# 126 tiny reads placed between the large loads of a memory-bound decode block

## The chip, the core and the metric

The kernel runs on one core of a Trainium2 chip. The metric is the device time of one execution in microseconds (us). Before the change it is 235.2 us, the median of two runs (235.15 and 235.26). Loads from the chip's memory (HBM) into the on-chip buffer are carried out by the core's 16 DMA engines; the engines that issue them here are SyncE (SP) and, for two small reads at the start, ScalarE (ACT). TensorE (PE) multiplies matrices, VectorE (DVE) transposes and does elementwise work, GpSimd (POOL) does a few copies.

## The reference

One decode step of a transformer block with modulation by a condition `c`, for a batch of 2, one new position each, model width 512, 32 query heads over 8 key/value heads of 128, the last W = 4096 positions of a cache of 32768, and a feed-forward width of 1792, all in float32:

```
mod = (silu(c) @ w_mod) in six parts sa, ca, ga, sb, cb, gb
h = layernorm(x) * (1 + ca) + sa
q = (h @ wq) as 32 heads;   k, v = k_cache, v_cache[:, :, 32768 - 4096 :, :]
p = softmax(q k^T / sqrt(128));   o = p v
x = x + ga * (o @ wo)
h = layernorm(x) * (1 + cb) + sb
x = x + gb * (silu(h @ w1) @ w2)
```

w_mod has 6 MB, wq 8 MB, the parts of the key and the value cache that are used 32 MB each, wo 8 MB, w1 and w2 3.5 MB each (MB here of 1024 KB). Every byte is used once.

## The kernel before

All operations are first recorded by `Flow.record`, which notes for each which earlier ones it depends on (by the regions of the on-chip tensors that it reads and writes); `Flow.emit` then issues them in the order in which they were written, each engine for itself, with a wait on a semaphore where a dependence needs one. Each DMA has its own semaphore, which is raised by 16 when it has landed. So the order of the loads is that of the code, on SP's queue, and a load whose buffer is still in use makes SP wait, and with it everything behind it on SP.

Nearly all loads go into one large tensor, `store`. Its first 32768 columns are four slots of 8192 (4 MB each). w_mod lies in slot 3 and the columns behind it, wq in slots 0 and 1. Keys and values come in eight steps t (four pairs of key/value heads by two batch rows, `seq`): the load k_t brings the keys of two heads, v_t the values, 4 MB each, with one packet of 32 KB to each of 128 partitions. The order of these sixteen loads is k0, k1, v0, k2, v1, k3, v2, ... k7, v6, v7 (`order`, line 470), and load i goes to slot (i + 2) mod 4 (`place`). `fetch(n)` issues the loads up to the n-th; the loop at line 487 calls it between the stages, so that a load is written behind the work that frees its slot:

```
for t in range(NP + 1):
    if t < NP:
        scores(t)          # DVE transposes k_t (4 x), PE multiplies, softmax
        fetch(max(5, 2 * t + 4))
    if t > 0:
        values(t - 1)      # PE multiplies the probabilities with v_(t-1)
        fetch(2 * t + 5)
    if t < NP:
        probabilities(t)
```

Behind the loop come wo in two parts (6 MB and 2 MB, called wo and wo2 below), w1 (3.5 MB) and w2 in four parts (2 MB, 1 MB and two of 256 KB). wo goes to slots 2 and 3, w1 to slot 0, w2 to slot 1. Their products (`product`, `narrow`) follow one another: o @ wo, the second layernorm, h @ w1, silu, the product with w2, and the store of the result.

At the end of `emit`, SP waits for all engines, clears the semaphores and waits for the last DMA.

Of the kernel before, what the change touches and what calls it, by code (L numbers as in the profile page):

```python
# [31 lines left out]
class Flow:  # L32
# [25 lines left out]
    def record(self, engine, method, args, kw):  # L58
        aps = [(k, v) for k, v in (*enumerate(args), *kw.items()) if isinstance(v, bass.AP)]
        outs = {0, "out", "accum_out"} if 0 in dict(aps) else {"out", "accum_out"}  # L60
        me = len(self.ops)
        needs = set()
        for writes in (False, True):
            for k, ap in aps:
                if (k in outs) != writes or "dram" in ap.tensor.name:
                    continue
                r = self.region(ap)
                held = self.seen.setdefault(ap.tensor.name, [])
                for other, w, o in held:
                    if (w or writes) and other != me and (  # L70
                        r[0] < o[1] and o[0] < r[1] and r[2] < o[3] and o[2] < r[3]
                    ):
                        needs.add((other, w))
                if writes:
                    held[:] = [
                        x for x in held
                        if not (r[0] <= x[2][0] and x[2][1] <= r[1] and r[2] <= x[2][2] and x[2][3] <= r[3])
                        or x[0] == me
                    ]
                held.append((me, writes, r))  # L80
        if engine == "pool":

            needs |= {(i, True) for i, o in enumerate(self.ops) if o[0] == "pool"}
        self.ops.append((engine, method, args, kw, needs))

    def emit(self):
        nc, ops = self.nc, self.ops
        proc = [("dma", i) if o[1] == "dma_start" else o[0] for i, o in enumerate(ops)]
        known = {e: {} for e in self.NAMES}
        after, waits, told = [], [], set()  # L90
        for i, (engine, method, _, _, needs) in enumerate(ops):
            mine, wait = known[engine], []
            for d, wrote in sorted(needs, reverse=True):
                p = proc[d]
                if p == engine and (engine == "pe" or not wrote):
                    continue
                if mine.get(p, -1) >= d:
                    continue
                wait.append(d)
                told.add(d)  # L100
                for q, n in after[d].items():
                    mine[q] = max(mine.get(q, -1), n)
                mine[p] = max(mine.get(p, -1), d)
            waits.append(wait)
            after.append(dict(mine))
        sems = {e: nc.alloc_semaphore(f"at_{e}") for e in self.NAMES}
        done = nc.alloc_semaphore("done")
        count = {e: 0 for e in self.NAMES}
        value, last = {}, None
        for i, (engine, method, args, kw, _) in enumerate(ops):  # L110
            eng = getattr(nc, self.NAMES[engine])
            for d in waits[i]:
                eng.wait_ge(*value[d])
            ins = getattr(eng, method)(*args, **kw)  # L114
            if method == "dma_start":
                last = nc.alloc_semaphore(f"dma{i}")
                ins.then_inc(last, 16)
                value[i] = (last, 16)
            elif i in told:
                count[engine] += 1  # L120
                ins.then_inc(sems[engine], 1)
                value[i] = (sems[engine], count[engine])

        for e in ("pe", "dve", "act", "pool"):
            getattr(nc, self.NAMES[e]).sem_inc(done, 1)
        nc.sync.wait_ge(done, 4)
        first = min(s.num for s in sems.values())
        nc.sync.sem_clear(range(first, last.num))
        nc.sync.wait_ge(last, 16)
        nc.sync.sem_clear(last)  # L130


def adaln_block(nc, x, k_cache, v_cache, wq, wo, w1, w2, c, w_mod, out):
# [7 lines left out]
    pe, dve, act, pool, sp = fl.pe, fl.dve, fl.act, fl.pool, fl.sp  # L141
# [6 lines left out]
    def buf(name, *shape):  # L148
        return nc.alloc_sbuf_tensor(name, list(shape), F32).ap()
# [36 lines left out]
    def load_cache(cache, t, where):  # L186
        hp, b = seq[t]
        sp.dma_start(
            where,
            cache[b, 2 * hp : 2 * hp + 2, SK - W :, :].rearrange(  # L190
                "u (i n) d -> i u (n d)", n=NK
            ),
        )
        return where
# [149 lines left out]
    for n in range(2):  # L344
# [4 lines left out]
        for g in range(G):  # L349
            r = slice(32 * g, 32 * g + 32)  # L350
            eng = pool if g % 2 else dve
# [7 lines left out]
        for i in range(4):  # L359
            r = slice(32 * i, 32 * i + 32)  # L360
# [115 lines left out]
    def fetch(n):  # L476
        for i in range(fetched[0], min(n, len(order))):
            what, t = order[i]
            if what == "k":
                kt[t] = load_cache(k_cache, t, place[i])  # L480
            else:
                vt[t] = load_cache(v_cache, t, place[i])
        fetched[0] = max(fetched[0], n)

    fetched = [0]
    fetch(4)
    for t in range(NP + 1):
        if t < NP:
            scores(t)
            fetch(max(5, 2 * t + 4))  # L490
        if t > 0:
            values(t - 1)
# [4 lines that stand above are left out]
    def load_rows(w, per, lo, hi, s, at):  # L497
        e = w.shape[1]
        n = (hi - lo) * e
        sp.dma_start(s[:, at : at + n], w.rearrange("(p q) e -> p (q e)", q=per)[:, lo * e : hi * e])  # L500
        v = s[:, at : at + n].rearrange("p (q e) -> p q e", e=e)
        return {q: v[:, q - lo, :] for q in range(lo, hi)}
# [2 lines left out]
    WIDE = 24  # L505
    for lo, hi in ((0, WIDE), (WIDE, 32)):
        wot |= load_rows(wo, 32, lo, hi, store[:, 2 * SLOT : 4 * SLOT], lo * D)
    w1t |= load_rows(w1, 4, 0, 4, slot[0], 0)
    for lo, hi in ((0, 8), (8, 12), (12, 13), (13, 14)):
        w2t |= load_rows(w2, T2, lo, hi, slot[1], lo * D)  # L510
# [143 lines left out]
```

## Time and profile before

| | |
|---|---|
| time, median of 2 runs | 235.2 us |
| profiled execution: whole time | 235.42 us |
| profiled execution: span from the first to the last instruction | 234.0 us |
| moved by DMA | 97.68 MB, 417 GB/s on the mean |
| busy share of the span: PE, DVE, ACT | 61%, 49%, 12% |
| chain of work that ended last: DMA, DVE, PE | 61%, 23%, 13% |

How to read it: the chain is followed back from the last instruction, at each step to what released it. A DMA's issue is an instruction of SP with a time of its own; its landing is seen when the semaphore is raised. "Packets" are the pieces that the DMA engines carried; the views on DMA count those under 512 bytes, under 2 KB and under 8 KB, and give the time that the packets of a queue took as a share of 16 engines' time in the window asked for. Queue q1 is SP's, q10 ACT's; q8 and q14 bring instructions. The packets carry no number of the engine that moved them.

### The profile page before, as it was taken

How to read it: one execution, taken by the hardware profiler on the slowest of the kernel's cores; microseconds unless marked ns; L12 is line 12 of the kernel's file. 1: busy time of each engine (PE TensorE's matmuls, PEld its weight loads, DVE VectorE, ACT ScalarE, POOL GpSimd, SP SyncE). 2: the span in 40 equal slices, each digit the busy share in tenths (PEclk: the TensorE clock that was granted, in tenths of full speed). 3: DMA queues.
4: the chain of work that ended last, by engine and by line, in shares of the span. 5: the costliest groups of instructions: out<-in, count | busy, mean ns of one | idle time of the engine just before them, and what ended most of it. 6: DMA issues, size and time to landing. Idle time of an engine off the chain costs nothing.

```text
span 234.0 us, 2450 instructions
## 1 busy us (share of the span) xinstructions
PE 143.0 (61%) x1070; PEld 41.8 (18%) x1070; DVE 113.9 (49%) x155; ACT 27.7 (12%) x62; POOL 8.1 (3%) x27
## 2 busy tenths in 40 slices
PE   0013905918458756995457755737664777859885
PEld 0001301211001200231100210200220022313425
DVE  4014100179497596794295477549429560200331
ACT  2003000010110120221200210120120030000500
POOL 4600000000000000000000000000000000000000
PEclk9999975895755997799955999797997697998999
DMA  7999998999999999999999999999999999989992
GB/s 269 438 516 392 403 493 358 445 431 420 426 433 437 437 434 420 431 423 437 448 420 420 434 431 437 437 416 431 428 448 431 426 442 437 437 384 447 407 412 79
DMA packets 3646, 97.68 MB, mean 417 GB/s; under 512 B 412, under 2 KB 436, under 8 KB 692
## 3 DMA queue, kind: packets, MB, share of 16 engines
q1 hardware_dynamic: 3612, 97.52, 97.3%
q8 instruction: 8, 0.13, 0.2%
q14 instruction: 2, 0.02, 0.0%
q10 hardware_dynamic: 24, 0.01, 0.0%
HBM read 97.53 MB, written 0.00 MB: 417 GB/s over the span
## 4 chain that ended last, share of the span: by engine, by line
DMA 61%; DVE 23%; PE 13%; issue 1%; ACT 1%; POOL 0%; SPq 0%; POOLq 0%
DMA store<-in_A_k_cache_dram 35%; DVE kT L114 19%; DMA store<-in_A_wq_dram 15%; DMA store<-in_A_wo_dram 11%; PE bankD L114 8%; PE bankA L114 3%; PE bankC L114 1%; DVE store L114 1%; PE bankB L114 1%; DVE qbd L114 0%; ACT store L114 0%; DVE wide L114 0%; DVE sgh L114 0%; DVE mx L114 0%; DVE hidT L114 0%
## 5 line engine op out<-in xcount | busy, mean ns | idle before, releaser
L114 DVE STREAM_TRANSPOSE kT<-store 128x2048 f32<-128x2048 f32 x32 | 71.1, 2279 | 15.6 <-DMA store<-in_A_k_cache_dram 15.5
L114 PE MATMUL bankA<-kT,qbd 128*32 128x512 f32 x256 | 49.6, 854 | 32.4 <-DVE kT L114 32.3
L114 PE MATMUL bankD<-store 128*32 128x512 f32 x256 | 33.7, 673 | 2.6 <-DMA store<-in_A_v_cache_dram 2.6
L114 PEld LDWEIGHTS bankA<-kT,qbd 128*32 128x32 f32 x256 | 6.2, 124 | 69.6 <-DVE kT L114 68.8
L114 PE MATMUL bankD<-store,hq_T 128*32 128x512 f32 x64 | 9.4, 752 | 8.6 <-DMA store<-in_A_wq_dram 8.6
L114 PEld LDWEIGHTS bankD<-store 128*32 128x32 f32 x256 | 8.6, 122 | 20.7 <-issue 20.6
L114 ACT COPY bias<-bankB 128x1 f32<-128x1 f32 x8 | 1.3, 159 | 91.4 <-PE bankB L114 91.4
L114 DVE STREAM_TRANSPOSE store<-store 128x512 f32<-128x512 f32 x8 | 5.7, 712 | 12.2 <-ACT store L114 12.2
L114 DVE TENSOR_REDUCE mx<-bankA 128x1 f32<-128x512 f32 x8 | 5.5, 692 | 12.2 <-PE bankA L114 12.2
L114 PE MATMUL bankB<-mv_a,avg 128*128 128x1 f32 x2 | 0.6, 363 | 16.7 <-DVE mv_a L114 16.7
L114 DVE TENSOR_TENSOR store<-store,half 128x512 f32<-128x512 f32 x16 | 10.3, 689 | 0.3
L114 DVE STREAM_TRANSPOSE wide<-bankD 128x512 f32<-128x512 f32 x2 | 1.4, 718 | 16.9 <-PE bankD L114 16.9
L114 PE MATMUL bankO<-store,pick 128*32 128x256 f32 x32 | 7.7, 382 | 2.9 <-ACT store L114 2.9
L114 PE MATMUL bankC<-store,sel 128*32 128x256 f32 x64 | 7.5, 414 | 3.1 <-DVE store L114 3.1
L114 ACT ACTIVATE store<-bankC,par 128x256 f32<-128x256 f32 x16 | 7.6, 475 | 10.9 <-PE bankC L114 10.7
L114 PE MATMUL bankD<-store,oTn 128*32 128x512 f32 x48 | 7.1, 750 | 2.9 <-DMA store<-in_A_wo_dram 2.9
L114 PE MATMUL bankC<-qbd,mean 128*128 128x512 f32 (+1 forms) x18 | 8.3, 591 | 0.0
L114 ACT COPY store<-bankD 128x512 f32<-128x512 f32 x8 | 4.7, 585 | 28.2 <-PE bankD L114 28.2
L114 DVE STREAM_TRANSPOSE aoT<-bankA 128x128 f32<-128x128 f32 x1 | 0.3, 316 | 14.0 <-PE bankA L114 14.0
L114 PE MATMUL bankB<-ident,mx 128*1 128x128 f32 x16 | 3.0, 271 | 6.5 <-DVE mx L114 6.5
L114 DVE BATCH_NORM_STATS2 st_a<-x_sp 128x6 f32<-128x128 f32 x1 | 0.3, 294 | 12.4 <-DMA x_sp<-in_A_x_dram 12.4
L114 PE MATMUL bankB<-negscale,mrow 1*128 1x1 f32 x16 | 3.4, 279 | 4.7 <-DVE mrow L114 4.7
(115 smaller groups left out, 91.0 us busy)
## 6 DMA issues: line engine op xcount, KB each, us to landing
store<-in_A_k_cache_dram SPq DMA_DIRECT2D x8, 4096.0 KB, 29.9
store<-in_A_v_cache_dram SPq DMA_DIRECT2D x8, 4096.0 KB, 29.0
store<-in_w_mod_dram SPq DMA_DIRECT2D x1, 6144.0 KB, 17.4
store<-in_A_wo_dram SPq DMA_DIRECT2D x1, 6144.0 KB, 25.0
store<-in_B_w_dram SPq DMA_DIRECT2D x1, 3584.0 KB, 30.8
store<-in_A_wo_dram SPq DMA_DIRECT2D x1, 2048.0 KB, 29.5
store<-in_B_w_dram SPq DMA_DIRECT2D x1, 2048.0 KB, 30.3
store<-in_B_w_dram SPq DMA_DIRECT2D x1, 1024.0 KB, 31.0
```

The costliest lines, as they stand in the source:

```text
L114: ins = getattr(eng, method)(*args, **kw)
```

## The change

A small tensor `small` of 16 partitions is added, and a function `read_small` that issues fourteen reads of the first words of `c` into it: the read with r rows (r = 2 to 15) brings r rows of r + 1 float32 words, so 12 to 64 bytes a row. Nothing reads `small`. The function is called nine times: in `fetch` after every second one of the sixteen loads of keys and values (after k1, k2, k3, ..., k7 and v7), and once between wo2 and w1. That makes 126 reads with 9 x 119 = 1071 rows, all on SP's queue.

The reads are kept out of the tracking of dependences (`record`) and share one semaphore, `tiny`. In `emit`, the first read of each group of fourteen, but for the first group, waits until all earlier tiny reads have landed; and at the end SP waits for all 126.

```diff
@@ record
-                if (k in outs) != writes or "dram" in ap.tensor.name:
+                if (k in outs) != writes or "dram" in ap.tensor.name or ap.tensor.name == "small":
@@ emit
+        tiny, tinies = nc.alloc_semaphore("tiny"), 0
...
             for d in waits[i]:
                 eng.wait_ge(*value[d])
+            if method == "dma_start" and args[0].tensor.name == "small" and tinies and tinies % 14 == 0:
+
+                eng.wait_ge(tiny, 16 * tinies)
             ins = getattr(eng, method)(*args, **kw)
-            if method == "dma_start":
+            if method == "dma_start" and args[0].tensor.name == "small":
+                ins.then_inc(tiny, 16)
+                tinies += 1
+            elif method == "dma_start":
...
         nc.sync.wait_ge(done, 4)
+        nc.sync.wait_ge(tiny, 16 * tinies)
@@ fetch
                 vt[t] = load_cache(v_cache, t, place[i])
+            if i % 2 == 1:
+                read_small(i // 2)
...
+    small = buf("small", 16, 14, 16)
+    cf = c.rearrange("b d -> (b d)")
+
+    def read_small(t):
+        for rows in range(2, 16):
+            n = 1 + rows
+            sp.dma_start(
+                small[:rows, rows - 2, :n],
+                cf[: rows * n].rearrange("(r n) -> r n", n=n),
+            )
@@ before w1
+    read_small(8)
     w1t |= load_rows(w1, 4, 0, 4, slot[0], 0)
```

On SP's queue, before, the part from k2 to k4 reads as follows (`store<-in_A_k_cache_dram` is a load of keys, `in_A_v_cache_dram` one of values; the shape is that of the target; a wait stands in brackets, `at_pe` and `at_dve` being the waits for PE and DVE to free the slot):

```order
5 L114 DMA store<-in_A_k_cache_dram 128x1x8192 [waits at_pe]
6 L114 DMA store<-in_A_v_cache_dram 128x1x8192 [waits at_dve]
7 L114 DMA store<-in_A_k_cache_dram 128x1x8192 [waits at_dve]
8 L114 DMA store<-in_A_v_cache_dram 128x1x8192 [waits at_pe]
9 L114 DMA store<-in_A_k_cache_dram 128x1x8192 [waits at_dve]
```

and now the part from the end of the group behind k2 to the first three reads of the group behind k3 (eleven more follow before v2):

```order
32 L118 DMA small<-in_c_dram 14x15
33 L118 DMA small<-in_c_dram 15x16
34 L118 DMA store<-in_A_v_cache_dram 128x1x8192 [waits at_dve]
35 L118 DMA store<-in_A_k_cache_dram 128x1x8192 [waits at_dve]
36 L118 DMA small<-in_c_dram 2x3 [waits tiny]
37 L118 DMA small<-in_c_dram 3x4
38 L118 DMA small<-in_c_dram 4x5
```

Between k3 and v2 (rows 7 and 8 before) there are now fourteen issues, and the first of them holds SP until the group behind k2 has landed; v2 and all later loads stand behind that wait. At the end of the loads SP had this before (`in_B_w_dram` is w1 in the first such row, then w2):

```order
18 L114 DMA store<-in_A_wo_dram 128x12288 [waits at_dve]
19 L114 DMA store<-in_A_wo_dram 128x4096
20 L114 DMA store<-in_B_w_dram 128x7168 [waits at_pe]
21 L114 DMA store<-in_B_w_dram 128x4096 [waits at_pe]
22 L114 DMA store<-in_B_w_dram 128x2048 [waits at_pe]
```

and has this now, up to the second read of the last group (twelve more follow, then w1):

```order
129 L118 DMA small<-in_c_dram 15x16
130 L118 DMA store<-in_A_wo_dram 128x12288 [waits at_dve]
131 L118 DMA store<-in_A_wo_dram 128x4096
132 L118 DMA small<-in_c_dram 2x3 [waits tiny]
133 L118 DMA small<-in_c_dram 3x4
```

w1 and w2 have moved behind the last group, whose first read waits for the group issued behind v7. On PE, DVE, ACT and POOL the instructions and their order are the same as before.

## The prediction

> **What bounds the kernel now.** I read the page's DMA part first, then the chain of waits, the windows around single loads, and SP's timeline. The page's part on DMA, with packets and megabytes by queue:
>
> ```profile
> DMA packets 3646, 97.68 MB, mean 417 GB/s; under 512 B 412, under 2 KB 436, under 8 KB 692
> q1 hardware_dynamic: 3612, 97.52, 97.3%
> q8 instruction: 8, 0.13, 0.2%
> q10 hardware_dynamic: 24, 0.01, 0.0%
> ```
>
> SP's queue keeps the 16 DMA engines busy for 97.3% of the span; there is almost nothing to win between loads. The chain (start, length, what):
>
> ```profile
> 74.64 22.65 DMA store<-in_A_k_cache_dram
> 106.22 29.93 DMA store<-in_A_k_cache_dram
> 183.95 25.01 DMA store<-in_A_wo_dram
> ```
>
> These give landings: k3 at 97.29, k5 at 136.15, wo at 208.96. From k3 to k5 four loads landed in 38.86 us, 9.72 us each, and 4.19 MB in 9.72 us is 432 GB/s. k5 was issued 29.93 us before its landing, three load times, so about two whole loads stood ahead of it: the ring never ran dry. At that pace wo's 6.29 MB took 14.6 us, so v7 landed at about 194.4; wo2 (2.10 MB, 4.9 us) at 213.8.
>
> The last wait for a load, from the timeline:
>
> ```profile
> 222.42 0.16 PEld L114 LDWEIGHTS bankA<-store,hT_b 128*32 128x32 f32 x8 [0.77 <-DMA store<-in_B_w_dram]
> ```
>
> PE waits for w1 at 222.42; from there to the end of the span are 11.6 us of dependent work. What delays w1's landing comes out at the end in full.
>
> A load lands when its latest engine has finished. Two windows of the DMA view, 16.85 to 17.76 us (the end of w_mod) and 191.5 to 194 us (the end of v7), show the completions, one small packet for each engine:
>
> ```profile
> DMA packets 32, 1.05 MB, mean 1152 GB/s; under 512 B 16, under 2 KB 16, under 8 KB 16
> ...
> DMA packets 46, 1.33 MB, mean 531 GB/s; under 512 B 16, under 2 KB 16, under 8 KB 16
> ```
>
> and the part of the second from 193 to 194 us holds five of them:
>
> ```profile
> DMA packets 16, 0.54 MB, mean 541 GB/s; under 512 B 5, under 2 KB 5, under 8 KB 5
> ```
>
> So all 16 finish w_mod within 0.91 us, but v7 only within 2.5 us, the last five in the last 1.0. The engines drift apart. The 8 instruction packets on q8 fit as one cause (0.2% of 16 x 234 us over 8 is 0.9 us each, on one engine at a time). Most engines are thus one to two microseconds early, and delay on those costs nothing.
>
> **The change part by part.** *Packets added.* A large load makes 128 + 16 packets: 25 x 144 = 3600 of q1's 3612; the remaining 12 are the result's store, eight rows with four completions, and q10's 24 are the reads of c and x, twice the same. A small DMA's rows thus come with fewer than 16 completions. I take a read of r rows as spread over r engines, with one data packet and one completion on each, a "pair". A group of fourteen then gives 14 pairs to an engine that every read touches, down to none for one that no read touches, 7.4 on the mean (119/16); nine groups give at most 126 and on the mean 67.
>
> *Price of a pair.* The trace has two nearby packets: a 4-byte completion (window 10.05 to 10.07 us) and a 512-byte row of c or x (window 6.38 to 6.40 us):
>
> ```profile
> q10 hardware_dynamic: 1, 0.00, 2.8%
> ...
> q10 hardware_dynamic: 1, 0.00, 8.4%
> ```
>
> 2.8% of 16 x 20 ns is 9 ns; 8.4% is 27 ns. The added rows have 12 to 64 bytes, nearer to 4 than to 512, so I take 9 ns, and 18 ns a pair; the ends are 0 (completions between large loads leave the pace at 432 GB/s) and 9 + 27 = 36 ns. On an engine with 126 pairs that is 2.3 us (0 to 4.5), with 67 pairs 1.2 us. Behind eight of the nine groups wo still waits; all nine precede w1.
>
> *What reaches the end.* If the latest engine carries none, the 2.3 us on the busiest one fit within the 2.5 us of spread: nothing. If the latest carries all 126, 2.3 us. The trace does not name engines. With 67 pairs on the latest it is 1.2 us, and as the second latest may carry more, I take 1.5 us. Below nothing: at best a delay of the early engines lets the late ones catch up, which is worth no more than the spread, 2.5 us.
>
> The Trainium skill (DMA: Bandwidth & Descriptors, "Anatomy of one DMA") speaks against the change: it gives every DMA a fixed cost of about 2.0 us. If that were paid in turn, 126 x 2.0 = 252 us would come on top, an estimate of 487 us by that page; the same section says that most of it is the wait for the write's receipt. The trace does not bear out a cost in turn: 25 large loads end in such a completion at an unbroken 432 GB/s.
>
> *SP's time.* Issues, from SP's timeline:
>
> ```profile
> 0.74 0.39 SPq L114 DMA_DIRECT2D store<-in_w_mod_dram  x1
> 74.64 0.54 SPq L114 DMA_DIRECT2D store<-in_A_k_cache_dram  x1
> 82.37 0.54 SPq L114 DMA_DIRECT2D store<-in_A_v_cache_dram  x1
> 232.24 0.69 SPq L114 DMA_DIRECT2D out_dram<-yo  x1
> ```
>
> and ACT's first, 1.12 us:
>
> ```profile
> 1.03 1.12 ACTq L114 DMA_DIRECT2D c_sp<-in_c_dram  x1
> ```
>
> At 0.54 us a group takes 14 x 0.54 = 7.6 us of SP (5.5 to 15.7 with 0.39 to 1.12). What is queued behind it: the next value load, and behind the last group w1 and w2. The group behind k3 waits for the one behind k2, which lands with k2 at 97.29 - 2 x 9.72 = 77.8. v2, issued at 82.37 before, is then issued at 77.8 + 7.6 = 85.4. The ring holds v1 and k3 until 97.29, so v2 is still 12 us early. All middle groups have this shape: the wait ends with two loads (19.4 us) left in the ring. The last waits for the group behind v7, until 194.4; then w1 is issued at 202.0 instead of 191.61, with wo and wo2 in the ring until 213.8. Cover: 19.4 us a group; without it, each microsecond of SP above that is a microsecond of idle DMA. It is gone above 19.4/14 = 1.39 us an issue, beyond the dearest row. So this term is nothing, and so is the wait on `tiny`. The group behind k1 has no wait; it fills time in which SP waits for PE until v0's issue at 45.29. The SP program grows from 25 to 151 DMAs, which may bring an instruction packet or two, 0.9 us on one engine: part of the range.
>
> *The sum*, on the profiled execution (235.42 us whole): 0 (SP) + 1.5 (pairs) = 236.9. The profile stands 0.2 above the median of 235.2, so 236.7 us.
>
> **The rivals.** (1) *No change:* the latest engine carries few of the pairs, or they slip in between large packets; under 0.5 us, 235.2 to 235.7. For: the spread, and the unbroken pace. Against: at most a few engines can be spared, and there are 16 to be missed.
>
> (2) *Slower: short packets do not stream.* Between large packets a small one may hide its handling behind a neighbour's data; here up to 28 follow one another. The nearest row with small packets in sequence is the tail of w2, window 230.1 to 230.6 us:
>
> ```profile
> DMA packets 16, 0.02 MB, mean 49 GB/s; under 512 B 4, under 2 KB 4, under 8 KB 16
> q1 hardware_dynamic: 16, 0.02, 13.1%
> ```
>
> 13.1% of 16 x 0.5 us is 1.05 us; less four completions at 9 ns, 12 packets of 2 KB took 84 ns each. If a tiny row cost that, a pair would be 93 ns and 126 of them 11.7 us: about 247 on the busiest engine, up to 2.5 less where it had been early. It decides the other way from 4.7/126 = 37 ns a pair if the latest engine carries all, from (4.7 + 2.5)/126 = 57 ns if it was the earliest. Typical, at 60 ns: 7.6 less 1.2 us of slack, 241.6. Against: 2 KB need most of those 84 ns for their bytes at 27 GB/s an engine (432/16), 76 ns, which leaves 8 ns for handling.
>
> (3) *The ring runs dry:* an issue of these reads costs more than 1.39 us. At 2.0 us a group takes 28 us, 8.6 more than its cover, for about eight groups: +69 us, 304. The dearest row, 1.12, speaks against it.
>
> (4) *In turn, or heaped:* each read holds its engine until it has landed. SP's own wait for the result's store, "SPq L130 <- DMA out_dram<-yo", shows such a time:
>
> ```profile
> SPq L130 <- DMA out_dram<-yo: 0.9, 1, 0.9
> ```
>
> 126 x 0.9 = 113 us, 348. Or a read is not spread by rows: then one engine gets 119 data packets and 14 completions a group, 9 x 133 x 9 ns = 10.8 us, about 245. The four completions of the store and of c and x speak against that. The Trainium skill (same page, "Why a DMA increments its semaphore by 16 and not by 1") spreads a DMA over the largest number of engines up to 16 that divides the row counts of both sides; the trace's fours agree with it, and no run here yet shows 2 to 15.
>
> (5) *Faster:* only by the spread, at most 2.5 us, which is 1%; a gain over 2% needs something that no row shows.
>
> **How the numbers follow.** Two runs of this kernel differ by 0.1 us; what a measurement tells from no change is taken as 2%, 4.7 us. Chances: forecast (0.5 to 4.5 us more) 0.51; (1) 0.26; (2) 0.15; (3) 0.02; (4) 0.03; (5) 0.03. Faster 0.03; same 0.51 + 0.26 = 0.77; slower 0.20. The range holds (1), the forecast with both its ends, and the nearer half of (2): from 235.0 to 241.5; outside lie (3), (4), (5) and the dear half of (2), 0.15 together.
>
> **What would show it.** Right: q1 with about 2100 packets more, nearly all under 512 bytes; four-load steps of the chain of 38.9 to 39.5 us; w1's wait on PE 0.5 to 4 us later than 222.42; SP's tiny issues at 0.4 to 0.7 us each, the DMA slices staying at 9. Wrong: gaps in the DMA slices behind k4 to wo (rival 3), tiny packets of 40 ns and more or idle time between them (rival 2), completions of one load spread over clearly more than 2.5 us, or a landing of k5 that has not moved while the end has.

## The result, and the profile after

The changed kernel takes 252.76 us (median of 2 runs, 252.63 to 252.89) against 235.2: a ratio of 1.073, 95% interval 1.068 to 1.078 (the quotient of the two medians is 1.075). One kernel's executions now and then run some per cent longer at a lower clock; all times here leave these out. The forecast was 236.7 us, the range 235.0 to 241.5; the time lies above the range, and beyond the 2% within which the likeliest case lay.

The page's packets, as before; then SP's wait for the tiny reads (time in all, times, longest); then the chain's three pieces and the last wait for a load that answer to those of before; then one group's issues in SP's timeline:

```profile
DMA packets 5789, 97.74 MB, mean 389 GB/s; under 512 B 2554, under 2 KB 2578, under 8 KB 2834
...
q1 hardware_dynamic: 5754, 97.58, 93.4%
```

```profile
SPq L118 <- DMA small<-in_c_dram: 101.4, 8, 15.1
```

```profile
74.31 25.45 DMA store<-in_A_k_cache_dram
108.69 33.55 DMA store<-in_A_k_cache_dram
194.56 28.77 DMA store<-in_A_wo_dram
```

```profile
239.72 0.16 PEld L118 LDWEIGHTS bankA<-store,hT_b 128*32 128x32 f32 x8 [1.51 <-DMA store<-in_B_w_dram]
```

```profile
144.79 4.91 SPq L118 DMA_DIRECT2D small<-in_c_dram  x14
```

q1 has 2142 packets more, as many as 1071 rows with a completion each. k3 lands at 99.76 instead of 97.29 (2.5 us late, two groups done), k5 at 142.24 instead of 136.15 (6.1, four groups), wo at 223.33 instead of 208.96 (14.4, eight groups), and PE waits for w1 until 239.72 instead of 222.42 (17.3, nine). So the time goes in the stream of loads, about 2 us a group once the first engines' slack is used, and the work behind w1's landing takes 11.6 us as before. The page's DMA slices still read 9 nearly throughout, up to the tail, so the 16 engines have not run dry together. But busy engines move less. These are the DMA view's rows from 100 to 180 us, of before and of the changed kernel: the packets fill the engines' time in both, and carry 33.3 MB now instead of 34.4, so time is lost within packets.

```profile
q1 hardware_dynamic: 1177, 34.37, 100.0%
q1 hardware_dynamic: 1974, 33.31, 100.5%
```

Where the 2 us are is seen on single engines. The small packets' sizes tell how many pairs an engine carried. These are rows of five windows of the DMA view in the group behind k6. The first (162.70 to 162.878 us) holds a whole run of 14 pairs. The other four are one to ten ns wide and hold the start of the first 32 KB packet behind a run of 5, 8, 11 and 14 pairs (from 153.773, 158.051, 161.254 and 162.877 us). The share times 16 times the window's width is the packet's time:

```profile
q1 hardware_dynamic: 29, 0.00, 9.7%
q1 hardware_dynamic: 1, 0.03, 7581.2%
q1 hardware_dynamic: 1, 0.03, 884.4%
q1 hardware_dynamic: 1, 0.03, 1207.5%
q1 hardware_dynamic: 1, 0.03, 1551.2%
```

The 14 pairs pass within 0.18 us: as packets they are as cheap as the prediction had them (9.7% of 16 x 178 ns over 29 is 9.5 ns). But the large packet behind them takes 75.81 x 16 x 1 = 1213 ns behind 5 pairs, its ordinary time, and 8.844 x 16 x 10 = 1415 ns behind 8, 1932 behind 11 and 2482 behind 14. From 8 to 14 that is 178 ns for each further pair, and in this packet it goes through nothing near seven.

The second large packet behind the run is long as well. These are the rows for the same four engines, in windows of 1 ns (from 154.982, 159.462, 163.182 and 165.359 us):

```profile
q1 hardware_dynamic: 1, 0.03, 8406.2%
q1 hardware_dynamic: 1, 0.03, 12443.8%
q1 hardware_dynamic: 1, 0.03, 11750.0%
q1 hardware_dynamic: 1, 0.03, 11150.0%
```

They took 1345, 1991, 1880 and 1784 ns. Both packets together are thus 0.13 us over their ordinary time behind 5 pairs, 0.98 behind 8, 1.39 behind 11 and 1.84 behind 14; the 0.18 us of the small packets makes it 2.0 us behind 14, which is a whole group's loss. The cost of the small reads stands in the two large packets that follow them.

### The profile page after: what moved, and what is told of

It reads as the page before. It is cut to its first block, busy times and chain, and to the rows that moved or that the text cites. A ratio compares the mean times of both kernels' runs of the same rounds, so it can differ in the third digit from the quotient of the medians.

```text
span 251.3 us, 2577 instructions
## 1 busy us (share of the span) xinstructions
PE 148.2 (59%) x1070; PEld 41.6 (17%) x1070; DVE 113.9 (45%) x155; ACT 27.8 (11%) x62; POOL 8.1 (3%) x27
## 4 chain that ended last, share of the span: by engine, by line
DMA 63%; DVE 21%; PE 13%; issue 1%; ACT 0%; POOL 0%; SPq 0%; POOLq 0%
DMA store<-in_A_k_cache_dram 37%; DVE kT L118 18%; DMA store<-in_A_wq_dram 14%; DMA store<-in_A_wo_dram 11%; PE bankD L118 8%; PE bankA L118 3%; PE bankC L118 2%; DVE store L118 1%; PE bankB L118 1%; DVE qbd L118 0%; ACT store L118 0%; DVE wide L118 0%; DVE sgh L118 0%; DVE mx L118 0%; DVE hidT L118 0%
## 5 line engine op out<-in xcount | busy, mean ns | idle before, releaser
L118 PE MATMUL bankA<-kT,qbd 128*32 128x512 f32 x256 | 52.4, 903 | 40.7 <-DVE kT L118 40.7
L118 PE MATMUL bankD<-store,oTn 128*32 128x512 f32 x48 | 8.3, 863 | 3.8 <-DMA store<-in_A_wo_dram 3.8
L118 PE MATMUL bankC<-qbd,mean 128*128 128x512 f32 (+1 forms) x18 | 10.0, 690 | 0.0
## 6 DMA issues: line engine op xcount, KB each, us to landing
store<-in_A_wo_dram SPq DMA_DIRECT2D x1, 2048.0 KB, 33.3
```

## The experiments

The theory (A): a short read costs the engine that carries it some 0.15 to 0.2 us in which it does not read ahead; a few in a row hide behind data that it has read already, the rest delays the next load; the engine with the most pairs sets the landing. Against it: the price is one of many rows read from the same bytes (B), of SP's wait (C), or of the pieces of data rather than of the reads (A1 against A2). The time of before is that of the runs beside each. Where the number of reads in a group changes (e2, e3, e6, e10), a wait still stands ahead of each group but the first; e5, e8, e11 and e12 have no waits between groups and read two words a row. The excerpts below leave such lines out.

**e1: two rows a read.** Two engines carry 14 pairs as before, the others none.

```diff
-        for rows in range(2, 16):
-            n = 1 + rows
-            sp.dma_start(small[:rows, rows - 2, :n], cf[: rows * n] ...)
+        for j in range(14):
+            n = 3 + j
+            sp.dma_start(small[:2, j, :n], cf[: 2 * n] ...)
```

> Every group keeps its fourteen reads, but each has 2 rows (of 3 to 16 words), so 28 rows a group instead of 119. Theory A (each short read costs an engine that carries a row of it about 0.17 us on its reading side; about 1.2 us of that, seven reads, hides behind data already read ahead; the latest engine sets the landing): two engines carry 14 pairs as before, so the time stays near the changed kernel's 252.8, 250 to 254. Theory B (the price comes from many rows read from the same few bytes of c, or from the number of small packets in all): a quarter of the rows, a quarter of the loss, 238 to 241. Theory C (the loss is SP's wait for the earlier group): the wait is unchanged, 250 to 254.

251.9 us against 235.5 (ratio 1.069, 1.058 to 1.080). A quarter of the rows costs as much: what counts is above all how many pairs the busiest engine has, not the packets in all. B falls. For the cost to be the same, the rows of all fourteen reads must share the same few engines. This agrees with the Trainium skill (DMA: Bandwidth & Descriptors, "Why a DMA increments its semaphore by 16 and not by 1"), by which a DMA that SP issues and that runs on fewer than 16 engines takes the lowest-numbered ones; no view here numbers them.

**e2: seven reads a group**, those with 9 to 15 rows.

```diff
-        for rows in range(2, 16):
+        for rows in range(9, 16):
```

> Every group has only the seven reads with 9 to 15 rows, so the busiest engines carry 7 pairs instead of 14. Theory A (about 0.17 us a read, seven of them hidden): almost nothing is left, 235.5 to 238. A price in proportion to the pairs with nothing hidden: half of the 17.6 us, 243 to 245. Theory C (SP's wait for the earlier group): the waits are as many as before, 249 to 253.

241.55 us against 235.54 (1.025, 1.021 to 1.029), 0.67 us a group. Neither nothing, as A had it, nor half: half the reads cost a third of the loss. Where it stands is seen on an engine with seven pairs in the group behind k6: these are the rows of the first and the second large packet behind them (windows of 1 ns from 158.140 and 159.354 us).

```profile
q1 hardware_dynamic: 1, 0.03, 7612.5%
q1 hardware_dynamic: 1, 0.03, 11162.5%
```

The first took its ordinary 1218 ns, the second 1786, which is 0.57 us too long; the small packets themselves add 0.1. Four more engines with seven pairs in this group have 1656 to 1991 ns in the second packet (from 156.594, 156.953, 157.913 and 158.339 us). The engine with seven pairs behind k6 in the changed kernel shows the same: 1222 ns (from 155.886 us), then 1647 (from 157.105 us).

**e3: one read a group with the same pieces.** Fifteen rows with fourteen separate runs of three words.

```diff
+        sp.dma_start(
+            small[:15, :, :3],
+            cf[:960].rearrange("(r j n) -> r j n", r=15, j=16)[:, :14, :3],
+        )
```

> Every group is one read of 15 rows with fourteen separate runs of three words in each, so an engine carries fourteen small data packets as before, but one completion. Theory A1 (the price is that of each small piece of data, read from memory): 14 pieces on fifteen engines, 250 to 256. Theory A2 (the price is that of each read's completion or of the start of each read): one a group, hidden, 235 to 237.

238.3 us (1.011, 1.007 to 1.016). Fourteen pieces on fifteen engines, with one completion, cost 0.31 us a group, against 1.95 for fourteen reads: the price is mostly that of a read, not of a piece of data. That is A2, though the time lies above its 235 to 237: the pieces are not quite free.

**e4: the source on the chip.** The shapes stay; the source is the identity matrix in the on-chip buffer.

```diff
-                cf[: rows * n].rearrange("(r n) -> r n", n=n),
+                ident[:rows, :n],
```

> The fourteen reads of a group keep their shapes, but their source is the identity matrix in the on-chip buffer instead of c in HBM. Theory A1 with the delay of an HBM read as its cause: on-chip reads are quicker, 235 to 240. Theory A2 (completions or starts): the same completions, 250 to 255. Theory B (all read the same few bytes of HBM): no HBM reads are left, 235 to 238.

250.9 us (1.065, 1.061 to 1.069). The delay of HBM is not the cause either.

**e5: no waits between groups**, each group with a piece of the tile of its own, two words a row.

```diff
-            if method == "dma_start" and args[0].tensor.name == "small" and tinies and tinies % 14 == 0:
-                eng.wait_ge(tiny, 16 * tinies)
...
-    small = buf("small", 16, 14, 16)
+    small = buf("small", 16, 9, 14, 2)
```

> As the changed kernel, but each group writes a piece of its own in the small tile (two words a row, so that it fits) and the waits between the groups are gone; only the one at the end is left. Theory A (about 0.19 us for each read on the engine that carries it, some 0.6 us of a group hidden): unchanged, 250 to 253. Theory C (SP held by the wait, and the loads behind it late): back to 235 to 238.

252.5 us (1.073, 1.067 to 1.079): the 101 us that SP waits for the tiny reads cost nothing, as the prediction had it. C falls. Its timeline, at the last wait for a load:

```profile
238.67 0.16 PEld L115 LDWEIGHTS bankA<-store,hT_b 128*32 128x32 f32 x8 [2.73 <-DMA store<-in_B_w_dram]
```

16.3 us later than before, without a single wait of SP for a tiny read.

**e6: three reads a group**, with 13 to 15 rows.

```diff
-        for rows in range(2, 16):
+        for rows in range(13, 16):
```

> Every group has only the three reads with 13 to 15 rows. Fourteen reads cost about 2.05 us a group, seven cost 0.7; a line through the two is 0.19 us a read less 0.63. By it three cost nothing, 235.2 to 236.2. If seven and fourteen lie on a curve through nothing instead (no part hidden, later reads dearer), three cost some 0.25 us a group, 237 to 238.

235.63 us against 235.25 (1.001, 0.998 to 1.004). Three in a row cost nothing that can be told from noise. At the last wait for a load:

```profile
222.87 0.16 PEld L118 LDWEIGHTS bankA<-store,hT_b 128*32 128x32 f32 x8 [1.06 <-DMA store<-in_B_w_dram]
```

**e7: the kernel before, its sixteen loads in eight parts each**, no tiny reads.

```diff
+        for part in range(8):
+            c0 = part * (SLOT // 8)
+            sp.dma_start(where[:, c0 : c0 + SLOT // 8], rows[:, :, c0 : c0 + SLOT // 8])
```

> The kernel before, with no tiny reads, but each of the sixteen loads of keys and values issued as eight loads of 512 KB, so that every engine gets 112 more reads with their completions, as the busiest engine did in the changed kernel (126), with 1.2 us of data between them. If the price is one of reads that stand back to back, so that nothing covers it: within 1% of before, 234 to 237.5. If each read costs its engine about 0.19 us wherever it stands: 112 x 0.19 = 21 us, 250 to 258.

245.3 us against 235.25 (1.043, 1.040 to 1.045): outside both expectations. The DMA view from 100 to 180 us:

```profile
DMA packets 8969, 32.72 MB, mean 409 GB/s; under 512 B 993, under 2 KB 993, under 8 KB 8964
q1 hardware_dynamic: 8964, 32.65, 102.4%
```

Its packets are 4 KB instead of 32 KB, and 16 x 80 us over 7971 of them is 160.6 ns each (completions included), against 4096 / 27 = 152 ns at before's pace. The 67.1 MB of keys and values at 409 instead of 432 GB/s take 164.1 instead of 155.3 us: 8.8 of the 10.1 us are the smaller packets' even pace, which the expectation had left out; the other 1.3 us stay open. There is no stall of 0.19 us a read.

**e8: the same loads in eight parts, a tiny read behind each of the first seven parts of every load**, so that no two stand together; two words a row, no waits, 112 reads (none ahead of w1).

```diff
             sp.dma_start(where[:, c0 : c0 + SLOT // 8], rows[:, :, c0 : c0 + SLOT // 8])
+            if part < 7:
+                read_small(part + 2 + 7 * (count[0] % 2))
```

> The loads split in eight as in the run beside it, and the fourteen tiny reads of a group (two words a row, no waits between groups) put one behind each of the first seven parts of two loads, so that no two stand together; the last group, ahead of w1, is left out, which makes 112 tiny reads. If the price is one of standing back to back: within 1% of the run with the split alone. If each tiny read costs its engine 0.19 us wherever it stands: 112 x 0.19 = 21 us above that run.

245.64 us, 0.33 more than e7, whose own runs lie between 244.5 and 245.6. The DMA view from 100 to 180 us:

```profile
DMA packets 9865, 32.58 MB, mean 407 GB/s; under 512 B 1925, under 2 KB 1925, under 8 KB 9860
```

112 tiny reads between other packets cost 3 ns each, if anything. The price is one of standing in a row.

**e9: sixteen rows a read**, so that all engines carry 14 pairs.

```diff
-        for rows in range(2, 16):
-            n = 1 + rows
-            sp.dma_start(small[:rows, rows - 2, :n], cf[: rows * n] ...)
+        for j in range(14):
+            n = 3 + j
+            sp.dma_start(small[:16, j, :n], cf[: 16 * n] ...)
```

> Every one of a group's fourteen reads has 16 rows (of 3 to 16 words), so that all 16 engines carry 14 pairs. If the engine that carries the most pairs sets the landing, the uneven load is no cost by itself: as the changed kernel, a little more as no engine is spared that was late already, 252 to 255. If the loss comes from the engines running apart (early engines idle while SP waits for the late ones), an even load gives most of it back: 238 to 245.

256.8 us (1.091, 1.084 to 1.098), a little above the first expectation: the uneven load is not the cause, and an even one is dearer, 2.4 us a group.

**e10: 28 reads of two rows a group.**

```diff
-        for rows in range(2, 16):
+        for j in range(28):
+            sp.dma_start(small[:2, j % 14, 8 * (j // 14) : 8 * (j // 14) + 3], cf[:6] ...)
```

> Every group has 28 reads of 2 rows, three words each. By the line through three, seven and fourteen reads (0.19 us a read less 0.63 a group) a group costs 4.7 us: nine of them 42 us, 274 to 279. If the cost of a group levels off (one refill of what the engine reads ahead, however long the pause), it stays near two to three microseconds a group: 253 to 262.

280.6 us against 235.2, from a single execution: 5.0 us a group, where the fourteen reads of two rows in e1 cost 1.8. The cost does not level off; it grows a little faster than the line.

**e11: seven reads behind every load**, 17 groups, 119 reads, two words a row, no waits between.

```diff
-            if i % 2 == 1:
-                read_small(i // 2)
+            read_small(i)
```

> Seven reads with 9 to 15 rows (two words each, no waits between) behind every one of the sixteen loads of keys and values and seven ahead of w1: 119 reads, nearly as many as in the changed kernel, never more than seven together. By the line, 17 groups at 0.7 us make 12 us: 246 to 248. If the number of reads decides and not how many stand together, 119/126 of the loss: 251 to 253. If what each group hides is all that matters and seven nearly fit in it: under 240.

248.4 us (1.056, 1.052 to 1.059), 0.78 us a group: dearer than the line's 246 to 248 by a little, and clearly cheaper than the same reads in groups of fourteen.

**e12: seven reads a group from ACT's queue.**

```diff
-            sp.dma_start(
+            act.dma_start(
```

> The seven reads of a group (9 to 15 rows, two words each, no waits between groups) issued from ACT's queue instead of SP's, at the same places of the program. If an engine takes packets of the two queues in turn, so that a large packet stands between two small ones, the price is covered as in the run with one tiny read behind each eighth of a load: 235 to 237. If seven reads cost their 0.7 us a group wherever they are queued: 241 to 242, as seven on SP's queue. Should ACT's own work be late by its seven issues of about 0.35 us, it would show as ACT on the chain of waits.

237.1 us (1.008, 1.006 to 1.009), 0.21 us a group instead of 0.67, just above the first expectation. The last wait for a load:

```profile
224.71 0.16 PEld L115 LDWEIGHTS bankA<-store,hT_b 128*32 128x32 f32 x8 [0.76 <-DMA store<-in_B_w_dram]
```

The whole of the loss still stands ahead of w1's landing (2.3 us later than before), so it is not in ACT's work behind that. The large and the small packets take turns, as far as the view tells: from 93.2 to 94.4 us, about the time of one large packet, the DMA view has 16 large packets on q1 and 10 small ones on ACT's q10.

```profile
q1 hardware_dynamic: 16, 0.52, 101.1%
q10 hardware_dynamic: 10, 0.00, 0.5%
```

That is fewer than one small packet to a large one, where fourteen pairs pass within 0.18 us on SP's queue. The second queue covers most of the price, not all.

The reads in a row put together, each against the before beside it:

| reads in a row | us a group | each further read |
|---|---|---|
| 3 (e6) | 0.04 | |
| 7 (e2) | 0.67 | 0.16 |
| 14 (the change) | 1.95 | 0.18 |
| 28 (e10) | 5.04 | 0.22 |

## Why the prediction was wrong

- *What bounds the kernel* held: the stream of loads up to w1's landing, and 11.6 us behind it.
- *Packets added* held: 2142 more, one data packet and one completion for each row.
- *SP's time* held as a term of nothing; an issue was sized too high, at 0.54 us instead of 0.35 (4.91 / 14). The wait on `tiny` is free, as e5 shows. Rival (3) did not come about.
- *The price of a pair* is the step that failed. It was taken as the time of two packets, 18 ns, with 36 as its upper end. The packets do take that time; but the engine pays for a short read elsewhere, in the two large packets that follow, and that is in no row of before, where no two short reads stand together between large ones. Measured, (252.76 - 235.2) / 126 is 139 ns a pair on the busiest engine, beyond the end of the range by nearly four times and beyond the 93 ns of the nearest row with small packets in sequence, w2's tail. A packet's own time was read as its whole cost.
- *What reaches the end* was the right rule (the latest engine) with a wrong choice that follows from the price. At 18 ns the 2.5 us of spread would have hidden most, and the latest engine need not have been a busy one; at 139 ns the busiest becomes the latest after a group or two and stays so. In the group behind v7 an early engine begins its first packet of wo at 195.65 us, while a late one, behind whose v7 a run of 14 pairs follows, begins its last packet of v7 at 205.2. These are the DMA view's rows for 195.653 to 195.660 us (that packet, and one small one) and for 205.203 to 205.213 us:

```profile
DMA packets 2, 0.05 MB, mean 7022 GB/s; under 512 B 1, under 2 KB 1, under 8 KB 1
...
DMA packets 1, 0.03 MB, mean 3277 GB/s; under 512 B 0, under 2 KB 0, under 8 KB 0
```

- *Rival (2)*, that a small packet hides its handling between large ones but not among its like, came nearest: e8 and e10 show both halves, and its deciding points (37 and 57 ns a pair) are far passed. The sign set down for it did not come, though: the tiny packets do stream, at 9 to 11 ns, and the delay stands behind them. The rival was priced at 60 ns and given 0.15, since the 2 KB row left only 8 ns for handling. That load has eight packets to a completion on each engine, and e3 shows that pieces which belong to one read are cheap.
- *Rival (4)*, each read in turn at 0.9 us, did not come about: even 28 reads in a row cost 0.2 us each, and between large packets 3 ns (e8). Nor did the 487 us by the fixed 2.0 us of the Trainium skill (DMA: Bandwidth & Descriptors, "Anatomy of one DMA"), paid in turn; that section is on DMAs that GpSimd issues, while SP issues these.
- *The signs set down.* The 2100 packets and the full slices came. The step from k3 to k5 took 42.48 us, beyond the 38.9 to 39.5, and the engines came to lie far more than 2.5 us apart at the end of a load, as said above.

What stays open: what in the engine takes the 0.16 to 0.22 us, the start of a read or its completion (every read has both, and no run here parts them). That it is time in which the engine does not read ahead, as A has it, would fit a delay that shows one and two large packets later, but is argued, not shown. Open too is why an even load is dearer (e9: 2.4 us a group instead of 1.95); that engines hinder each other in this was not tried by itself.

## What to carry to other kernels

A packet's duration in a trace is not the price of a small DMA: look at the large packets behind it, the second too, and at landings further on. In a kernel bound by its loads, small DMAs on the loads' queue are free while they stand one by one, or up to three together, between large packets; in a row each costs its busiest engine about 0.2 us, and reads of few rows fall on the same engines (e1). Spread them between the loads, or put them on the other queue, which covered two thirds of the price here.

## What had not been expected of the hardware

With an on-chip source (e4) SP needs twice as long to issue the same fourteen reads. SP's timeline of e4, to be held against the 4.91 us above:

```profile
144.16 10.66 SPq L118 DMA_DIRECT2D small<-ident  x14
```

That is 0.76 us a read instead of 0.35, hidden here like the rest of SP's time (250.9 us against the changed kernel's 252.8). And loads in 4 KB packets run at 409 GB/s, 5% below those in 32 KB packets, and evenly so (e7).
